# Weight pieces gated by landings, two-tile MLP groups, loads spread over a round and split transposes in a fused attention and MLP kernel

## The chip, the cores and the metric

The kernel runs on one core of one Trainium2 chip. The metric is the device time of one execution in microseconds (us), measured outside the profiler. Ratios below are the mean time of one kernel's fast runs over that of the other kernel's fast runs of the same rounds on the same chip, so they are not quite the ratio of the medians that I quote. A run counts as slow when it lies more than 1.5% above the fastest run of its kernel on that chip; slow runs are in the medians but not in the ratios. A point below is one per cent of before's time. Profiles are single executions; their span (253.97 us before) is some 1.7 us shorter than the device time of the same execution (255.67 us). So the profiled execution of before lay 1.7 us above the median of its runs.

In the lines of profiles PE is TensorE's matmuls, PEld its weight loads, DVE VectorE, ACT ScalarE, POOL GpSimd; SPq and ACTq are SyncE and ScalarE issuing transfers, and L92 is line 92 of that kernel. A bracket gives the idle time before an instruction and what ended it. A transfer lands when the engines that wait for it may go on. The granted clock is the share of TensorE's full clock in the profile's records, which begin 19.3 us into the span before; where there is no record it is printed as full.

## The reference, cut to what matters

A decaying linear attention over 4 batches, 8 heads, 768 positions and head size 64 (float32), and then, on its output x of 3,072 rows by 512, a normalization and a two-layer MLP with a residual:

```python
# attention, per block of 64 positions, state carried from block to block
intra = einsum('bhic,bhjc->bhij', qb, kb) * Dmask          # decayed causal mask
out   = einsum('bhij,bhjd->bhid', intra, vb) + einsum('bhid,bhde->bhie', qb * lam_pow, kv_state)
kv_state = lam_block * kv_state + einsum('bhsd,bhse->bhde', kb * rev_pow, vb)
...
# MLP on x = out, laid out as (batch, position, head*dim)
xn = (x - mean) / sqrt(var + 1e-6) * g_ln
y  = x + maximum(xn @ w_ch1, 0) @ w_ch2                    # 512 -> 2048 -> 512
```

## The kernel before

The work is cut into 12 *windows* of 256 rows (two tiles of 128), with the four batches in turn. For each window SyncE loads k, q and v (512 KB each), mostly GpSimd turns k, q and v into bf16 (q and v scaled), k and q are transposed (`kqT`; by TensorE in the first three windows, by a transposing DMA afterwards), TensorE makes the state products (`pk`), the scores (`sc`) and the attention output (`po`), VectorE and ScalarE normalize it (`x`, `xc`), `xc` is transposed (`xT`), and the MLP runs on *groups* of tiles. The weights come as eight pieces, four of each layer, through GpSimd's queue, which turns float32 into bf16 on the way (before's page: 4.19 MB moved by that queue, for 8.39 MB of float32 weights).

```python
def load_window(u, after_pool=False, parts=1):      # all three loads of a window at once, on SyncE
    ...
def load_w1(c): nc.gpsimd.dma_start(w1[c], ...)     # one piece of the first layer's weights
def load_w2(c): nc.gpsimd.dma_start(w2[c], ...)
...
sizes = [2, 2, 2, 2, 2, 2, 4, 4, 4]                 # tiles of each MLP group
...
# the front: order in which weights and windows are asked for
load_w1(0); load_window(1, after_pool=True); ...
load_w1(1); load_w1(2); ... in_q(1, nc.gpsimd); in_v(1, nc.gpsimd)
load_w1(3); load_window(2, after_pool=True); load_w2(0)
...
load_w2(1); load_w2(2); load_w2(3)                  # issued a few us later, long before window 2 is needed
...
# the plan: a list of MLP steps (first layer: 8 or 4 matmuls, second layer: 4), with attention put in between
def s1_s3(u):                                       # one round: state products and scores of u, output of u-1
    kv(u); scores(u, 0); av(u - 1, range(NP)); inter(u - 1, 0, fence=False)
    new_state(u, 0, nc.gpsimd); mask(u, 0); reader(u - 1); new_state(u, 1, nc.gpsimd)
def ahead_of(u):
    for f, w in ((transpose_dma, u + 1), (load_window, u + 3), (p0, u + 2)): ...   # p0: GpSimd's preparation
for at, j, rest in ((40, 5, 4), (56, 6, 4), (65, 7, 4), (73, 8, 4), ...):
    after[at] = [(s1_s3, j)]
    after[at + rest] = [(s2_s4, j), (p4, j - 1)]    # p4: the x transposes of window j-1
    after[at - 1] = [(ahead_of, j)]
```

## Time and profile before

| | before |
|---|---|
| device time, median of 3 | 253.99 us (253.97 to 254.61) |
| TensorE busy / idle until its last matmul | 212.4 us / 36 us |
| TensorE takes up q of window 2 | 48.47 us |
| round 6 starts | 117.24 us |
| last matmul ends | 248.3 us |
| mean granted clock of TensorE | 0.941 |

The row "takes up q" is the start of the run of seven transposes after the wait for window 2's q:

```profile
48.47 0.93 PE L183 MATMUL tp<-ident,kq 128*128 128x128 bf16 x7 [0.71 <-POOL kq L169]
```

A round is the attention work put in between the MLP steps for one window; round 6 is that of window 6. From the place above on, the order of the MLP steps is the same in both kernels up to round 6. The other lines stand in the prediction.

### The profile page before, as it was taken

Reading aid. Unit: us, or ns where it says so; the run is one execution under the profiler, and the core shown is the slowest. Engines: PE = TensorE matmul, PEld = TensorE weight load, DVE = VectorE, ACT = ScalarE, POOL = GpSimd, SP = SyncE. Lnnn points to the kernel's source line nnn. Section 1 sums busy time; section 2 is a strip of 40 time slices with the busy share of each in tenths; the row PEclk is TensorE's granted clock in tenths of the full one; section 3 lists DMA queues with packets and bytes.
Section 4 is the critical chain, followed back from the end, with each engine's and each line's share of the span. In section 5 each row is a group of like instructions: output and inputs, shape, how many; then the busy total and the mean of one; then the engine's idle time right before and its main releaser. Section 6 shows DMA issues by size and latency. Waiting matters only on the chain.

```text
span 254.0 us, 6453 instructions
## 1 busy us (share of the span) xinstructions
PE 212.4 (84%) x2829; PEld 123.9 (49%) x2848; DVE 101.7 (40%) x216; ACT 85.0 (33%) x154; POOL 74.2 (29%) x92
## 2 busy tenths in 40 slices
PE   1664892499999949699978996989999899999991
PEld 0454681364476437448546742545445444444440
DVE  2762431037535712354558271261562605300121
ACT  5446174131035003313504511462115632067000
POOL 5705600538608456461073725000000000000000
PEclk9999799579999967799999997999999999999998
DMA  5997799579799989986999999326043110430042
GB/s 155 239 259 138 118 207 218 124 197 290 127 270 245 264 150 317 229 119 103 211 193 235 243 265 151 61 43 85 18 108 85 24 23 9 116 83 3 0 108 57
DMA packets 75276, 37.38 MB, mean 147 GB/s; under 512 B 30960, under 2 KB 72176, under 8 KB 75248
## 3 DMA queue, kind: packets, MB, share of 16 engines
q1 hardware_dynamic: 70880, 32.78, 61.6%
q0 software_dynamic: 4224, 4.19, 10.1%
q8 instruction: 22, 0.36, 0.6%
q14 instruction: 6, 0.05, 0.1%
q10 hardware_dynamic: 144, 0.00, 0.0%
HBM read 27.53 MB, written 6.29 MB: 133 GB/s over the span
## 4 chain that ended last, share of the span: by engine, by line
PE 54%; DMA 24%; POOL 8%; DVE 5%; SPq 4%; issue 2%; ACT 1%; DVEq 0%; ACTq 0%; POOLq 0%
PE pm L383 26%; PE pm L357 22%; DMA qin<-in_q_dram 10%; DMA vin<-in_v_dram 10%; POOL vb L174 3%; DMA kin<-in_k_dram 3%; POOL kq L169 2%; DMA xT<-xc 2%; SPq L189 2%; SPq L75 2%; PE po L270 2%; DVE stats L307 2%; PE sc L205 2%; POOL Sn L235 1%; DVE xc L309 1%
## 5 line engine op out<-in xcount | busy, mean ns | idle before, releaser
L357 PE MATMUL pm<-xT,w 128*128 128x256 bf16 (+1 forms) x539 | 93.6, 332 | 9.4 <-DMA xT<-xc 5.5
L383 PE MATMUL pm<-w,hT 128*128 128x512 bf16 x370 | 85.3, 380 | 1.1 <-issue 0.5
L360 ACT ACTIVATE hT<-pm 128x512 bf16<-128x512 f32 x92 | 53.6, 597 | 82.0 <-PE pm L357 81.9
L357 PEld LDWEIGHTS <-w 128*128 128x128 bf16 x544 | 55.0, 105 | 42.1 <-DMA xT<-xc 6.4
L383 PEld LDWEIGHTS <-hT 128*128 128x128 bf16 x384 | 36.7, 98 | 42.8 <-issue 0.6
L404 DVE SCALAR_TENSOR_TENSOR o<-pm,rstd,x 128x512 f32<-128x512 f32 (+1 forms) x25 | 18.0, 725 | 48.0 <-PE pm L383 31.2
L215 DVE TENSOR_TENSOR mA<-sc,keep 128x512 bf16<-128x512 f32 x44 | 28.2, 682 | 22.5 <-PE sc L205 22.4
L169 POOL TENSOR_TENSOR kq<-qin,lam_q 128x512 bf16<-128x512 f32 (+1 forms) x24 | 24.0, 1019 | 27.2 <-DMA qin<-in_q_dram 27.1
L235 POOL TENSOR_TENSOR Sn<-Stmp,lam_s 128x256 bf16<-128x256 f32 x16 | 9.8, 612 | 60.0 <-DVE Stmp L239 51.3
L174 POOL TENSOR_TENSOR vb<-vin,lam_v 128x1024 bf16<-128x1024 f32 (+1 forms) x13 | 23.1, 1782 | 7.2 <-DMA vin<-in_v_dram 7.2
L307 DVE BATCH_NORM_STATS2 stats<-x 128x6 f32<-128x512 f32 x20 | 13.8, 691 | 21.3 <-ACT x L305 21.2
L183 PE MATMUL tp<-ident,kq 128*128 128x128 bf16 x48 | 6.4, 279 | 16.9 <-POOL kq L169 8.3
L305 ACT COPY x<-po 128x512 f32<-128x512 f32 x20 | 10.9, 590 | 28.3 <-PE po L283 23.7
L309 DVE SCALAR_TENSOR_TENSOR xc<-po,mv,g_row 128x512 bf16<-128x512 f32 x24 | 18.0, 750 | 2.0
L239 DVE TENSOR_TENSOR Stmp<-pk,Sn 128x256 f32<-128x256 f32 x16 | 6.7, 418 | 27.6 <-PE pk L229 20.8
L161 POOL CAST kq<-kin 128x512 bf16<-128x512 f32 x16 | 9.3, 611 | 22.4 <-DMA kin<-in_k_dram 22.4
L183 PEld LDWEIGHTS <-kq 128*128 128x128 bf16 x48 | 4.0, 122 | 18.8 <-DVE kq L161 9.4
L270 PE MATMUL po<-vb,mA 64*64 64x64 bf16 x768 | 10.3, 199 | 1.9 <-issue 1.3
L205 PE MATMUL sc<-kqT 64*64 64x128 bf16 x352 | 10.0, 227 | 1.5 <-ACT kqT L184 0.9
L270 PEld LDWEIGHTS <-mA 64*64 64x64 bf16 x768 | 9.0, 110 | 3.5 <-issue 2.6
L184 ACT COPY kqT<-tp 128x1024 bf16<-128x1024 bf16 (+1 forms) x7 | 5.7, 830 | 13.7 <-PE tp L183 13.7
L334 ACT ACTIVATE std<-mv,eps_t 128x2 f32<-128x2 f32 x12 | 3.6, 298 | 19.7 <-DVE mv L308 19.7
(54 smaller groups left out, 90.3 us busy)
## 6 DMA issues: line engine op xcount, KB each, us to landing
kin<-in_k_dram SPq DMA_DIRECT2D x11, 512.0 KB, 5.4
qin<-in_q_dram SPq DMA_DIRECT2D x11, 512.0 KB, 6.2
vin<-in_v_dram SPq DMA_DIRECT2D x11, 512.0 KB, 8.0
out_dram<-o SPq DMA_DIRECT2D x22, 256.0 KB, 3.5
w<-in_moe_w_ch_dram POOLq DMA_DIRECT2D x8, 512.0 KB, 11.3
kin<-in_k_dram SPq DMA_DIRECT2D x2, 256.0 KB, 4.7
qin<-in_q_dram SPq DMA_DIRECT2D x2, 256.0 KB, 5.1
vin<-in_v_dram SPq DMA_DIRECT2D x2, 256.0 KB, 5.4
```

What stands on the lines that cost most here:

```text
L169: eng.tensor_tensor(dst[:, :, :, j], src[:, :, :, j], lq[:, :, :, j:j + 1].to_broadcast([128, n, 2, D]), op=ALU.mult)
L174: eng.tensor_tensor(st[u]["vb"][:, hs], qkv_in[u]["v"][:, hs], lam_v[:, hs, :, None].to_broadcast([128, n, 2, D]), op=ALU.mult)
L205: nc.tensor.matmul(sc[e][half[ab], i, jk, :], lhsT=kT[half[e], 2 * hf + i, jk, half[ab]], rhs=qT[half[e], 2 * hf + i, :, half[ab]], start= ...
L215: nc.vector.tensor_tensor(s[f"mA{hf}"][:, e], s[f"sc{hf}"][e], kp[:, None, :, :].to_broadcast([128, 2, 2, 128]), op=ALU.mult)
L235: eng.tensor_tensor(dst, src, lam_s[:, :, None].to_broadcast([128, NP, D]), op=ALU.mult)
L270: nc.tensor.matmul(s["po"][ab][half[jq], 2 * p + e, :], lhsT=s[f"mA{p // 2}"][half[ab], e, p % 2, j, half[jq]], rhs=s["vb"][half[ab], 2 * ...
L307: nc.vector.bn_stats(stats, po if early else x)
L309: nc.vector.scalar_tensor_tensor(xc, in0=po, scalar=mv[:, 0:1], in1=g_row, op0=ALU.subtract, op1=ALU.mult)
L357: nc.tensor.matmul(pm[:, b, :], lhsT=w1[n // W2K][:, kk, (n % W2K) * 128:(n % W2K + 1) * 128], rhs=xT_of[g][:, kk, 0:N], start=(b == 0 and ...
L360: nc.scalar.activation(hT[:, u * NB:(u + 1) * NB, 0:N], pm, ACT.Relu)
L383: nc.tensor.matmul(acc[i], lhsT=hT[:, kk, i * 128:(i + 1) * 128], rhs=w2[kk // W2K][:, kk % W2K, :], start=(kk == 0), stop=(kk == KB - 1))
L404: nc.vector.scalar_tensor_tensor(o[:, ab, sl], in0=a[:, sl], scalar=rstd[:, ab:ab + 1], in1=x[:, ab, sl], op0=ALU.mult, op1=ALU.add)
```

## The change

Its intent is to have neither weights nor inputs wait for the other in the first 50 us, and to have nothing wait in the rounds. Cut to its core:

```diff
-    sizes = [2, 2, 2, 2, 2, 2, 4, 4, 4]
+    sizes = [2] * NU                                  # and GT = 2
@@ the front
+    def behind(tile_ap):                              # GpSimd reads one column of a tile: it waits for its landing
+        seen_p = wk.tile([128, 1], F32, tag="seen_p", name="seen_p")
+        nc.gpsimd.tensor_copy(seen_p, tile_ap)
     open_window(0)
-    load_w1(0)
-    load_window(1, after_pool=True)
+    load_window(1)
...
+    behind(w1[0][:, 0, 0:1])
     load_w1(1)
+    in_q(1, nc.gpsimd)
     load_w1(2)
+    load_w1(3)
     in_v(1, nc.gpsimd)
+    load_w2(0)
+    behind(w1[2][:, 0, 0:1])
     load_window(2, after_pool=True)
...
-    load_w2(1)
-    load_w2(2)
-    load_w2(3)
+    behind(w2[0][:, 0, 0:1])
+    load_w2(1)
+    in_q(2, nc.gpsimd)
+    load_w2(2)
+    in_v(2, nc.gpsimd)
+    load_w2(3)
@@ k and q transposed by two DMAs
-        nc.sync.dma_start_transpose(s["kqT"]..., s["kq"]...)
+        for a in range(2):
+            nc.sync.dma_start_transpose(s["kqT"][:, a]..., s["kq"][:, a]...)
@@ the rounds
+    for j in range(6, NU):
+        at = 56 + 16 * (j - 6)
+        add(at - 1, (transpose_dma, j + 1))
+        add(at, (s1_s3, j))
+        add(at + 2, (p0, j + 2))                      # behind the state sums of round j, no longer in front
+        add(at + 4, (s2_s4, j), (p4, j - 1))
+        for n, name in zip((3, 7, 10), "kqv"):
+            add(at + n, (load_one, j + 3, name))      # one load at a time
@@ the tail: the last tile's second layer in two halves of columns, each stored on its own,
@@ the stores from SyncE and ScalarE
```

(Cut: rounds 2 to 5, which are spread in the same way by hand; the first window's order; in the rounds, the second state sum ahead of the second half of the mask.)

More of the change, by code (lines that the diff above doesn't have):

```diff
@@ L39 @@
     KB = DF // 128
-    GT = 4
+    GT = 2
     NWC = 4
@@ L64, in source, with load_one @@
         return src[b, hs, cc * W:(cc + 1) * W, :].rearrange("h (p j) d -> p h (j d)", j=2)
+    def load_one(u, name):
+        got = inp.tile([128, H, 2 * D], F32, tag=name + "in", name=name + "in")
+        nc.sync.dma_start(got, source(dict(k=k, q=q, v=v)[name], u, slice(0, H)))
+        qkv_in.setdefault(u, {})[name] = got.rearrange("p h (j d) -> p h j d", j=2)
     def load_window(u, after_pool=False, parts=1):
@@ L128 @@
     lam_v = const.tile([128, H, 2], F32)
-    for j in range(2):
-        nc.scalar.activation(lam_v[:, :, j], lnlam, ACT.Exp, scale=e_v[:, j:j + 1])
     lam_c = const.tile([128, H], F32)
-    nc.scalar.activation(lam_c, lnlam, ACT.Exp, scale=float(C))
     lam_s = const.tile([128, NP], F32)
@@ L188, in transpose_dma @@
         s["kqT"] = wk.tile([128, 2, NP, 2, 128], BF16, tag="kqT", bufs=3, name="kqT")
-        nc.sync.dma_start_transpose(s["kqT"].rearrange("p a b j t -> p (a b j) t"),
-                                    s["kq"].rearrange("p a b j e d -> p (a b j e d)"))
+        for a in range(2):
+            nc.sync.dma_start_transpose(s["kqT"][:, a].rearrange("p b j t -> p (b j) t"),
+                                        s["kq"][:, a].rearrange("p b j e d -> p (b j e d)"))
     def scores(u, hf, early=False):
@@ L209, in scores, with mask @@
         s[f"sc{hf}"] = sc
-    def mask(u, hf):
+    def mask(u, hf, heads=(0, 1)):
         s = st[u]
         kp = keep.rearrange("p a b t -> p a (b t)")
-        for e in range(2):
+        for e in heads:
             nc.vector.tensor_tensor(s[f"mA{hf}"][:, e], s[f"sc{hf}"][e],
@@ L345, in mlp @@
         N = n_t * 128
-        NB = max(1, GT // n_t)
+        NB = 4 // n_t
         def m1(u):
@@ L379, in m2 @@
             t = groups[g][i]
+            if t == 2 * NU - 1:
+                w = DM // 2
+                if part % 2 == 0:
+                    acc[i] = mm_tile([128, w], F32, "pm2h")
+                z = part // 2
+                for kk in range(part % 2 * 8, part % 2 * 8 + 8):
+                    nc.tensor.matmul(acc[i], lhsT=hT[:, kk, i * 128:(i + 1) * 128],
+                                     rhs=w2[kk // W2K][:, kk % W2K, z * w:(z + 1) * w],
+                                     start=(kk == 0), stop=(kk == KB - 1))
+                if part % 2 == 1:
+                    finish_half(t, acc.pop(i), z, w)
+                return
             if part == 0:
@@ L398, in finish, with finish_half @@
         rows = out[b, cc * W:(cc + 1) * W, :].rearrange("(c p j) d -> j p c d", c=2, j=2)
-        last = u == NU - 1
-        n_p = 2 if last and ab == 1 else 1
-        w = DM // n_p
-        for z in range(n_p):
-            sl = slice(z * w, (z + 1) * w)
-            nc.vector.scalar_tensor_tensor(o[:, ab, sl], in0=a[:, sl], scalar=rstd[:, ab:ab + 1], in1=x[:, ab, sl],
-                                           op0=ALU.mult, op1=ALU.add)
-            if last:
-                for j in range(2):
-                    nc.sync.dma_start(rows[j][:, ab, sl], o[half[j], ab, sl])
-        if ab == 1 and not last:
+        nc.vector.scalar_tensor_tensor(o[:, ab], in0=a, scalar=rstd[:, ab:ab + 1], in1=x[:, ab],
+                                       op0=ALU.mult, op1=ALU.add)
+        if u == NU - 1:
+            for j in range(2):
+                nc.sync.dma_start(rows[j][:, ab], o[half[j], ab])
+        elif ab == 1:
             for j in range(2):
                 nc.sync.dma_start(rows[j], o[half[j]])
-    sizes = [2, 2, 2, 2, 2, 2, 4, 4, 4]
+    def finish_half(t, a, z, w):
+        u, ab = divmod(t, 2)
+        x, rstd = x_keep[u]
+        cc, b = divmod(u, B)
+        o = o_of[u]
+        sl = slice(z * w, (z + 1) * w)
+        rows = out[b, cc * W:(cc + 1) * W, :].rearrange("(c p j) d -> j p c d", c=2, j=2)
+        nc.vector.scalar_tensor_tensor(o[:, ab, sl], in0=a, scalar=rstd[:, ab:ab + 1], in1=x[:, ab, sl],
+                                       op0=ALU.mult, op1=ALU.add)
+        for j, eng in enumerate((nc.sync, nc.scalar)):
+            eng.dma_start(rows[j][:, ab, sl], o[half[j], ab, sl])
+    sizes = [2] * NU
     groups = [list(range(sum(sizes[:i]), sum(sizes[:i + 1]))) for i in range(len(sizes))]
@@ L423 @@
     HA, HB = slice(0, 4), slice(4, 8)
+    def behind(tile_ap):
+        seen_p = wk.tile([128, 1], F32, tag="seen_p", name="seen_p")
+        nc.gpsimd.tensor_copy(seen_p, tile_ap)
     open_window(0)
-    seen_k = const.tile([128, 1], F32)
-    nc.gpsimd.tensor_copy(seen_k, qkv_in[0]["k"][:, 0, 0, 0:1])
-    load_w1(0)
-    load_window(1, after_pool=True)
-    in_k(0, nc.vector, HA)
-    transpose_pe(0, 0, (0, 1), nc.vector)
-    nc.vector.tensor_tensor(lam_q[:, :, 1], lam_q[:, :, 0], lam_b, op=ALU.mult)
-    in_q(0, nc.gpsimd, HA)
-    in_k(0, nc.vector, HB)
+    load_window(1)
+    in_k(0, nc.vector, HA)
+    transpose_pe(0, 0, (0, 1))
+    for j in range(2):
+        nc.scalar.activation(lam_v[:, :, j], lnlam, ACT.Exp, scale=e_v[:, j:j + 1])
+    nc.scalar.activation(lam_c, lnlam, ACT.Exp, scale=float(C))
+    nc.vector.tensor_tensor(lam_q[:, :, 1], lam_q[:, :, 0], lam_b, op=ALU.mult)
+    in_q(0, nc.vector, HA)
+    in_k(0, nc.gpsimd, HB)
+    load_w1(0)
     in_q(0, nc.vector, HB)
+    transpose_pe(0, 0, (2, 3), nc.vector)
     lam_cp = lam_c.rearrange("p (a two) -> p a two", two=2)
@@ L438 @@
         nc.vector.tensor_copy(lam_s[half[e]], lam_cp[half[e], :, e])
+    transpose_pe(0, 1, (0, 1))
+    transpose_pe(0, 1, (2, 3))
+    sqrt_first = const.tile([128, 1], F32)
+    nc.scalar.activation(sqrt_first, eps_t, ACT.Sqrt)
     in_v(0, nc.gpsimd, HA)
     in_v(0, nc.gpsimd, HB)
-    transpose_pe(0, 0, (2, 3))
-    transpose_pe(0, 1, (0, 1))
     scores(0, 0)
     mask(0, 0)
-    transpose_pe(0, 1, (2, 3))
+    scores(0, 1, early=True)
+    mask(0, 1)
     kv(0)
-    scores(0, 1, early=True)
     new_state(0, 0, nc.gpsimd)
-    mask(0, 1)
-    sqrt_first = const.tile([128, 1], F32)
-    nc.scalar.activation(sqrt_first, eps_t, ACT.Sqrt)
     av(0, (0, 1, 2))
@@ L455 @@
     av(0, (3,), (0,))
+    open_window(1)
+    norm(0, 0, early=True)
+    behind(w1[0][:, 0, 0:1])
     load_w1(1)
+    in_q(1, nc.gpsimd)
     load_w1(2)
-    open_window(1)
-    in_k(1, nc.scalar)
-    norm(0, 0, early=True)
-    in_q(1, nc.gpsimd)
+    load_w1(3)
     in_v(1, nc.gpsimd)
-    load_w1(3)
+    load_w2(0)
+    behind(w1[2][:, 0, 0:1])
     load_window(2, after_pool=True)
-    load_w2(0)
     m1a, m2a = mlp(0)
@@ L475 @@
     to_xT(0, 0)
+    in_k(1, nc.scalar)
     inter(0, 1)
     norm(0, 1, early=True)
-    transpose_pe(1, 0, (0, 1, 2, 3))
-    keep_x(0, (0,))
     m1a.tile(0, 0)
     to_xT(0, 1)
+    transpose_pe(1, 0, (0, 1, 2, 3))
     transpose_pe(1, 1, (0, 1, 2, 3))
+    m1a.tile(0, 1)
+    keep_x(0, (0,))
     keep_x(0, (1,))
-    m1a.tile(0, 1)
     scores(1, 0)
@@ L488 @@
     mask(1, 1)
-    load_w2(1)
-    load_w2(2)
-    load_w2(3)
+    rstd_of(0)
+    m1s(m1a, 1)
     kv(1, "po")
@@ L494 @@
     st[1]["tmp"] = state_sum(1, 1)
-    rstd_of(0)
-    m1s(m1a, 1)
     av(1, (0, 1, 2, 3))
@@ L502 @@
     norm(1, 1, early=True)
-    open_window(2)
-    in_k(2, nc.vector)
-    in_q(2, nc.gpsimd)
-    in_v(2, nc.gpsimd)
-    load_window(3, after_pool=True)
-    load_window(4)
     m1s(m1a, 2, 1, 2)
@@ L513 @@
     m1s(m1a, 3, 1, 2)
+    open_window(2)
+    in_k(2, nc.vector)
     m1b.tile(0, 0)
@@ L517 @@
     rstd_of(1)
+    behind(w2[0][:, 0, 0:1])
[4 more added lines that the diff above has]
+    load_w2(3)
+    load_window(3, after_pool=True)
+    load_window(4)
     def p0(u, k_eng=None):
@@ L537, in s1 @@
         new_state(u, 0, nc.gpsimd)
-        mask(u, 0)
+        mask(u, 0, (0,))
         new_state(u, 1, nc.gpsimd)
+        mask(u, 0, (1,))
     def s2(u):
@@ L568, in s1_s3 @@
         new_state(u, 0, nc.gpsimd)
-        mask(u, 0)
+        mask(u, 0, (0,))
+        new_state(u, 1, nc.gpsimd)
+        mask(u, 0, (1,))
         reader(u - 1)
-        new_state(u, 1, nc.gpsimd)
     def s2_s4(u):
@@ L588 @@
         plan += [(m2, i, part) for i in range(len(groups[g])) for part in range(KB // 4)]
-    def ahead_of(u):
-        for f, w in ((transpose_dma, u + 1), (load_window, u + 3), (p0, u + 2)):
-            if w < NU:
-                f(w)
-    after = {0: [(transpose_pe, 2, 0, (0, 1, 2, 3))], 1: [(transpose_pe, 2, 1, (0, 1, 2, 3))],
-             2: [(new_state, 0, 1, nc.gpsimd), (new_state, 1, 1, nc.gpsimd)],
-             4: [(s1b, 2)], 5: [(s0, 2)], 6: [(s2, 2)], 7: [(p0, 3, nc.vector)], 9: [(s3, 2)], 11: [(s4, 2), (p4, 2), (transpose_dma, 3), (load_window, 5)],
-             17: [(p0, 4)], 24: [(s1, 3)], 26: [(transpose_dma, 4), (load_window, 6), (s2, 3)],
-             28: [(s3, 3), (p0, 5)], 30: [(s4, 3), (p4, 3)], 33: [(s1, 4)], 35: [(transpose_dma, 5), (load_window, 7)], 36: [(s2, 4)],
-             37: [(p0, 6)]}
@@ L602, with add @@
-    for at, j, rest in ((40, 5, 4), (56, 6, 4), (65, 7, 4), (73, 8, 4), (89, 9, 4), (105, 10, 4), (121, 11, 4)):
-        after[at] = [(s1_s3, j)]
-        after[at + rest] = [(s2_s4, j), (p4, j - 1)]
-        after[at - 1] = [(ahead_of, j)]
-    after[135] = [(s3, 11)]
-    after[139] = [(s4, 11), (p4, 11)]
+    after = {}
+    def add(at, *steps):
+        after.setdefault(at, []).extend(steps)
+    add(0, (transpose_pe, 2, 0, (0, 1, 2, 3)))
+    add(1, (transpose_pe, 2, 1, (0, 1, 2, 3)))
+    add(2, (new_state, 0, 1, nc.gpsimd), (new_state, 1, 1, nc.gpsimd))
@@ new lines @@
+    add(4, (s1b, 2))
+    add(5, (s0, 2))
+    add(6, (s2, 2))
+    add(7, (p0, 3, nc.vector))
+    add(9, (s3, 2))
+    add(11, (s4, 2), (p4, 2), (transpose_dma, 3))
+    for n, name in zip((12, 14, 16), "kqv"):
+        add(n, (load_one, 5, name))
+    add(17, (p0, 4))
+    add(24, (s1, 3))
+    add(26, (s2, 3))
+    add(26, (load_one, 6, "k"))
+    add(28, (s3, 3), (p0, 5))
+    add(29, (s4, 3), (p4, 3), (transpose_dma, 4))
+    add(31, (load_one, 6, "q"))
+    add(32, (load_one, 6, "v"))
+    add(37, (transpose_dma, 5))
@@ new lines @@
+    add(38, (load_one, 7, "k"))
+    add(41, (s1, 4))
+    add(42, (p0, 6))
+    add(43, (s2, 4), (load_one, 7, "q"))
+    add(45, (s3, 4), (load_one, 7, "v"))
+    add(46, (s4, 4), (p4, 4))
+    add(46, (transpose_dma, 6))
+    add(50, (s1, 5))
+    add(51, (p0, 7))
+    add(52, (s2, 5))
+    for n, name in zip((48, 50, 52), "kqv"):
+        add(n, (load_one, 8, name))
+    for j in range(6, NU):
+        at = 56 + 16 * (j - 6)
+        if j + 1 < NU:
+            add(at - 1, (transpose_dma, j + 1))
+        add(at, (s1_s3, j))
+        if j + 2 < NU:
+            add(at + 2, (p0, j + 2))
+        add(at + 4, (s2_s4, j), (p4, j - 1))
+        if j + 3 < NU:
+            for n, name in zip((3, 7, 10), "kqv"):
+                add(at + n, (load_one, j + 3, name))
@@ L608 @@
+    add(150, (s3, NU - 1))
+    add(154, (s4, NU - 1), (p4, NU - 1))
     for i, (f, *a) in enumerate(plan):
```

## The prediction

Marked cuts below are clauses that gave rules of the hardware without a trace that shows them; what was measured beside them stays. The sum: 254.0 - 12.8 - 6.8 + 1.2 - 1.9 = 233.7. Two terms in it are my estimates, and before's trace has for them: 1.6 us from the end of the last packet (252.3) to the end of the span for the "some 1.5" of a landing, and 2.75 us from the end of the last issue (251.2) for the "about 2.5" of the tail. The 2,048 bytes read per weight packet are the float32 weights, 8.39 MB of the 27.53 MB on the page's HBM line, over 4,096 packets.

> **What bounds the kernel now.** I read the page's busy line, its table of 40 slices, then the chain of waits in order of time, the waits of TensorE, the issue queue of SyncE, and last the windows.
>
> ```profile
> PE 212.4 (84%) x2829; PEld 123.9 (49%) x2848; DVE 101.7 (40%) x216; ACT 85.0 (33%) x154; POOL 74.2 (29%) x92
> PE   1664892499999949699978996989999899999991
> PEclk9999799579999967799999997999999999999998
> DMA  5997799579799989986999999326043110430042
> ...
> q1 hardware_dynamic: 70880, 32.78, 61.6%
> q0 software_dynamic: 4224, 4.19, 10.1%
> ```
>
> One slice is 6.35 us. Counted from 0, TensorE is full in most slices but not in the first eight and not in 14, 16 and 24. The DMA row is well filled from the start to slice 24 and loose afterwards: up to about 159 us two resources share the bound, from then on TensorE alone has it. The chain of waits names the two long front waits, window 1's v and window 2's q:
>
> ```profile
> 7.86 16.21 DMA vin<-in_v_dram
> ...
> 27.33 18.96 DMA qin<-in_q_dram
> 46.29 0.07 issue
> 46.37 2.06 POOL kq L169 x2
> ...
> 117.31 0.44 PE pk L229 x32
> ```
>
> An undisturbed q load takes 6.2 us from issue to landing (median of the page); this one took 19. All five remaining weight pieces had been issued with it, four of them just behind:
>
> ```profile
> 26.77 0.12 POOL L70 MEMSET kin<- 128x1 f32 x1
> 26.81 2.97 POOL L87 DMA_DIRECT2D w<-in_moe_w_ch_dram  x4
> 46.37 2.05 POOL L169 TENSOR_TENSOR kq<-qin,lam_q 128x512 bf16<-128x512 f32 x2 [16.58 <-DMA qin<-in_q_dram]
> ```
>
> TensorE waits 6.1 us for that q (until 47.47). The windows, by stretch, give the rest (columns: stretch, length, busy of PE, PEld, DVE, ACT, POOL with counts, granted clock, DMA share, GB/s):
>
> ```profile
> 85.00:93.00 8.00, 4.72 (x36) 2.17 (x36) 3.78 (x7) 0.00 (x0) 6.21 (x7) 0.88 1.36 217
> 93.00:104.00 11.00, 8.93 (x176) 6.81 (x175) 2.19 (x6) 3.58 (x6) 5.91 (x7) 0.78 1.09 238
> 121.00:137.00 16.00, 14.22 (x265) 8.91 (x265) 9.71 (x21) 4.12 (x9) 6.30 (x7) 1.00 1.27 200
> 137.00:155.00 18.00, 14.40 (x220) 9.06 (x219) 10.20 (x22) 6.00 (x12) 9.67 (x11) 1.00 1.16 242
> 172.00:220.00 48.00, 46.98 (x574) 22.79 (x579) 20.81 (x44) 14.34 (x28) 1.22 (x2) 1.00 0.26 57
> ```
>
> Length minus PE busy is TensorE's idle time: 3.28, 2.07, 1.78, 3.60, 1.02 us here, 0.22 in 104 to 121 and 0.71 in 155 to 172. Sum after 85 us: 12.7. A DMA share above 1 stands beside all four large gaps, and 0.26 beside the small one, so those look like waits for traffic or for what is queued behind it.
>
> [...] q of window 2, on SyncE's queue, took 18.96 us beside GpSimd's weights. [...] A weight packet here carries 1,024 written bytes (2,048 read), an input packet 512; [...] in the packet records a quarter-megabyte of input took about 3.6 us while weights ran, 0.9 us alone. [...] 24 matmuls of 256 columns took 5.30 us after the wait at 92 us, 2.62 us warm at 71 us. [...] 226 ns for 512 columns, 109 to 116 for 256.
>
> **The change part by part.**
>
> 1. *Front.* Before, GpSimd issues w1's pieces 1 and 2 at 10.8 us, beside window 1, and five pieces around window 2. Now window 1 is issued at once, w1(1) only after w1(0) has landed, w1(2), w1(3), w2(0) among q and v of window 1; window 2 follows the landing of w1(2); w2(1) follows the landing of w2(0), w2(2) the q and w2(3) the v of window 2. Eight weight pieces take 10.1% of 254 = 25.7 us of all engines, 3.2 us each; input packets 73.0 us by the packet records, 6.1 per window. Estimate: w1(0) lands at about 16, w1(1) 22, w1(2) 27.5. So window 2 is issued near 28, hardly earlier than the 26.9 of before, but beside two pieces (7 us) rather than five (16). Its q then lands near 39.5; GpSimd takes 2.05 us. TensorE resumes at about 41.5 instead of 48.5: **-7.0 us at that place**.
>
> 2. *Is that gain kept?* This is the step in which I chose. From there to round 6 (its state products run at 117.3 us in the chain) the DMA engines carry nearly as much as TensorE. Their work ahead of round 6: eight windows 48.7, g_row 1.0, weights 25.7, four k/q transposes at 3.74 = 15.0 and six x transposes at 0.94 = 5.6 (28,672 packets hold 52.4 us), six outputs at 0.98 = 5.9 (23.4 us over 24): 101.9, from about 2.5 us on, plus some 1.5 for the last landing: 106. TensorE alone, from 41.5: before it needed 117.3 - 48.5 = 68.8, of which 0.8 + 0.3 + 3.3 + 2.1 + 0.2 = 6.7 idle and about 3.5 at half clock: 58.6, so round 6 at about 100. The truth lies between, since not all of that traffic has to be in front and the transposes' average includes congestion: I take 104.5. **-12.8 us** in all up to there, the 7.0 included.
>
> 3. *Rounds 6 to 11.* Before: 1.78 + 3.60 + 0.71 + 1.02 = 7.1 us idle, and 1.7 at half clock (16 matmuls in 5.30 us at 154.8 instead of 3.61). The groups of four needed two windows' xT at once; groups of two need one and come ten steps of 0.9 us after its transposes. Loads are issued one at a time; the GpSimd work of window j+2 stands behind the state sums of round j rather than in front, where it held the sum for a late v (1.90 us at 131.50, with 0.58 behind it). By step 2's terms a window needs 6.1 + 3.7 + 1.9 + 2.0 = 13.7 us of DMA against some 16.4 of TensorE (7.4 + 6.9 for the group, 2.1 attention), so DMA no longer limits. Recovered 8.8 less 2.0 that I leave for waits on xT (half the slack of nine us is the normalization on VectorE and ScalarE): **-6.8**.
>
> 4. *Costs of two-tile groups.* 192 matmuls of 512 columns become 384 of 256: 192 x (2 x 116 - 226) = **+1.2**. Weight loads (98 ns) stay beside matmuls of 109 or more. The relu has as many instructions as before, 0.6 us per 0.9 of TensorE.
>
> 5. *Tail.* TensorE ends at 248.3, the program at 254.0: two VectorE halves, four issues one after another on SyncE (2.38), landing. Now half the last tile leaves before the last sixteen matmuls, and the last two issues are on two queues: 0.48 + 0.55 + about 2.5 rather than 5.7. Less 0.25 for halving the last matmuls: **-1.9**. Splitting the k and q transposes adds nine issues on SyncE, which isn't the bound: 0.
>
> Sum: 254.0 - 12.8 - 6.8 + 1.2 - 1.9 = 233.7; I say **233.5**.
>
> **The rivals.** (a) DMA stays the bound to round 6. For it: share 0.9 to 1.36 there, and the 101.9 us of traffic, of which the change removes nothing. Then round 6 starts at 106 to 108 and the time is 236 to 238. (b) DMA hides entirely and TensorE is fed from 41.5: 229. (c) A new wait takes the old one's place: GpSimd, in program order, now stops for landed weights in front of in_q, in_v and the states; a late v of window 2 would hold back w2(3) and window 3 after it, and the second layer waits on weights. Against it: w2(3) would land near 53, and the first product that needs it comes near 57. It would give back 4 to 8 us: 238 to 242. (d) Rounds of 16 short steps are too tight for xT, 1 to 2 us of wait in each of six rounds: 236 to 242. Before, from the end of the state products at 181.8 to the landed xT was 7 us, under the nine now given, which speaks against it.
>
> **Range and chances.** (b) with a good tail gives 227, (a) and part of (d) 241: range **227 to 241**. To miss 2% (248.9) both the front and the gaps must fail, against a visible 18.96 us wait and 12.7 us of idle TensorE. Faster **0.94**, same **0.05**, slower **0.01**.
>
> **What would show it.** Step 1: the wait for window 2's q under 13 us, TensorE back at 41 to 42. Step 2: round 6's state products near 104; at 100 the DMA was no bound, at 108 it was the only one. Step 3: under 3 us of TensorE idle from there to its last matmul, clock 1.00 throughout. Step 4: TensorE's 256-column matmuls 110 to 116 ns apart, warm. Step 5: under 4 us from the last matmul to the end. I am wrong if GpSimd shows long waits for w, if second-layer matmuls wait for a weight piece, or if xT waits appear in every round.

## The result, and the profile after

The changed kernel takes 230.3 us (median of 4, 229.45 to 231.11) against 253.98 (median of 4, 252.61 to 254.61). The ratio of the fast runs is 0.907, 95% interval 0.902 to 0.913. I had said 233.5, range 227 to 241.

The page of the changed kernel, the same rows that the prediction shows of before:

```profile
PE 204.7 (89%) x3056; PEld 139.4 (61%) x3056; DVE 101.4 (44%) x216; ACT 84.9 (37%) x154; POOL 73.4 (32%) x93
PE   0647697989999999698999999999999999999992
PEclk9999999999999999999999999999999999999999
DMA  5996999999999999999999699695193212311303
```

Counted from 0, TensorE is full from slice 9 on but for slices 16 and 18 and the last. It does the same arithmetic in 7.7 us less busy time, mainly because the clock row has no dip any more (mean 1.00 instead of 0.941). That holds from the first clock record on: before it, 16 matmuls of 128 columns at 18.15 us take 1.89 us, against 1.06 at 21.63. The DMA row has lost its dips too: it is full from slice 4 to 21, then loose.

The chain of waits, columns start, length, what (the first two against 27.33 to 46.37 of before, the last against 117.31):

```profile
27.69 9.36 DMA qin<-in_q_dram
...
37.12 2.05 POOL kq L171 x2
...
100.30 0.38 PE pk L232 x32
```

Window 2's q was issued no earlier than before (27.69 against 27.33 us), but was there after 9.4 us rather than 19. What GpSimd does in between, from its timeline, shows why; the weight pieces w2(1) to w2(3) are the lines of L92:

```profile
33.51 0.74 POOL L92 DMA_DIRECT2D w<-in_moe_w_ch_dram  x1 [0.27 <-issue]
37.12 2.05 POOL L171 TENSOR_TENSOR kq<-qin,lam_q 128x512 bf16<-128x512 f32 x2 [2.87 <-DMA qin<-in_q_dram]
39.12 0.80 POOL L92 DMA_DIRECT2D w<-in_moe_w_ch_dram  x1
39.95 1.91 POOL L176 TENSOR_TENSOR vb<-vin,lam_v 128x1024 bf16<-128x1024 f32 x1
41.80 0.80 POOL L92 DMA_DIRECT2D w<-in_moe_w_ch_dram  x1
```

One piece goes out after w2(0) has landed, one after q, one after v. In the packet records w2(1) moves its first packet at 36.3 us, when q is practically in (its last packets start at 35.0). TensorE takes up q here:

```profile
39.23 0.56 PE L185 MATMUL tp<-ident,kq 128*128 128x128 bf16 x7 [0.78 <-POOL kq L171]
```

The stretches of TensorE (stretch, length, busy of PE, PEld, DVE, ACT, POOL with counts, granted clock, DMA share, GB/s). First of the kernel before, from q of window 2 on:

```profile
48.50:59.00 10.50, 10.45 (x116) 6.79 (x118) 4.01 (x8) 3.40 (x5) 5.20 (x7) 0.76 0.66 172
71.20:97.40 26.20, 22.86 (x331) 14.85 (x335) 12.04 (x23) 7.44 (x13) 12.16 (x14) 0.88 1.10 243
97.40:117.30 19.90, 17.61 (x264) 11.76 (x267) 8.12 (x17) 5.93 (x11) 11.02 (x12) 0.90 0.93 183
117.30:248.40 131.10, 123.78 (x1532) 64.36 (x1544) 52.08 (x111) 44.61 (x83) 20.09 (x23) 0.99 0.55 105
```

and of the changed kernel:

```profile
49.40:60.80 11.40, 10.31 (x55) 4.53 (x52) 6.23 (x13) 0.89 (x3) 7.86 (x8) 1.00 1.17 254
80.70:100.30 19.60, 17.42 (x321) 10.88 (x324) 11.35 (x23) 5.55 (x10) 12.42 (x14) 1.00 1.22 221
117.30:149.90 32.60, 32.20 (x501) 21.76 (x502) 15.61 (x33) 11.85 (x22) 11.81 (x13) 1.00 0.96 178
149.90:182.20 32.30, 32.08 (x482) 21.52 (x484) 15.19 (x32) 11.85 (x22) 6.21 (x7) 1.00 0.64 90
182.20:224.90 42.70, 42.53 (x521) 29.54 (x520) 13.87 (x30) 15.21 (x28) 0.61 (x1) 1.00 0.23 55
```

From 117 us on TensorE idles 0.40 + 0.22 + 0.17 us in 108 us. What idle time is left lies in front: 15.1 us in the first 39.3, 1.1 and 2.2 us in the first two stretches above, and 1.0 us at 106.3.

The account by milestones. Each interval is taken between the same two places of the program:

| interval | before | after | change |
|---|---|---|---|
| start to q of window 2 taken up | 48.5 | 39.2 | -9.2 |
| from there to the start of round 6 | 68.8 | 61.0 | -7.8 |
| round 6 to the last matmul's end | 131.1 | 124.6 | -6.5 |
| last matmul's end to the end of the span | 5.6 | 4.1 | -1.6 |
| span | 254.0 | 228.9 | -25.1 |

(The medians differ by 23.7 us only, since the profiled execution of before was slower than its median.)

The tail, from the timelines; before:

```profile
248.33 0.88 DVE L404 SCALAR_TENSOR_TENSOR o<-pm,rstd,x 128x256 f32<-128x256 f32 x2 [2.70 <-PE pm L383]
248.84 2.38 SPq L408 DMA_DIRECT2D out_dram<-o  x4
```

after:

```profile
223.65 2.25 ACTq L433 DMA_DIRECT2D out_dram<-o  x2
224.88 0.48 DVE L430 SCALAR_TENSOR_TENSOR o<-pm2h,rstd,x 128x256 f32<-128x256 f32 x1 [1.26 <-PE pm2h L389]
```

One half of the last tile is added and stored while the other is still being multiplied, so one VectorE step and half of the stores follow the last matmul instead of two and all. No run undoes the tail alone; its share is read from these profiles.

### The profile page after: what moved, and what is told of

It reads as the page before. It is cut to its first block, busy times and chain, and to the rows that moved or that the text cites. A ratio compares the mean times of both kernels' runs of the same rounds, so it can differ in the third digit from the quotient of the medians.

```text
span 228.9 us, 6911 instructions
## 1 busy us (share of the span) xinstructions
PE 204.7 (89%) x3056; PEld 139.4 (61%) x3056; DVE 101.4 (44%) x216; ACT 84.9 (37%) x154; POOL 73.4 (32%) x93
## 3 DMA queue, kind: packets, MB, share of 16 engines
HBM read 27.53 MB, written 6.29 MB: 148 GB/s over the span
## 4 chain that ended last, share of the span: by engine, by line
PE 52%; DMA 24%; POOL 8%; issue 6%; DVE 5%; ACT 2%; SPq 1%; DVEq 0%; POOLq 0%
PE pm L360 24%; PE pm L398 22%; DMA w<-in_moe_w_ch_dram 7%; DMA qin<-in_q_dram 6%; DMA kin<-in_k_dram 6%; POOL kq L171 3%; DMA xT<-xc 2%; DMA kqT<-kq 2%; DVE stats L310 2%; POOL kq L163 2%; POOL vb L176 2%; PE po L273 2%; PE pm2h L389 2%; DVE xc L312 1%; PE pk L232 1%
## 5 line engine op out<-in xcount | busy, mean ns | idle before, releaser
L360 PE MATMUL pm<-xT,w 128*128 128x256 bf16 x736 | 87.3, 273 | 3.4 <-DMA xT<-xc 1.3
L363 ACT ACTIVATE hT<-pm 128x512 bf16<-128x512 f32 x92 | 54.6, 596 | 91.7 <-PE pm L360 91.6
L398 PE MATMUL pm<-w,hT 128*128 128x512 bf16 x368 | 83.0, 379 | 0.4
L360 PEld LDWEIGHTS <-w 128*128 128x128 bf16 x736 | 69.8, 98 | 15.7 <-issue 3.0
L398 PEld LDWEIGHTS <-hT 128*128 128x128 bf16 x368 | 34.9, 98 | 41.6 <-ACT hT L363 2.6
L414 DVE SCALAR_TENSOR_TENSOR o<-pm,rstd,x 128x512 f32<-128x512 f32 x23 | 17.1, 745 | 35.4 <-PE pm L398 35.2
L171 POOL TENSOR_TENSOR kq<-qin,lam_q 128x512 bf16<-128x512 f32 x22 | 22.6, 1048 | 10.4 <-DMA qin<-in_q_dram 10.2
L185 PE MATMUL tp<-ident,kq 128*128 128x128 bf16 x48 | 5.3, 261 | 8.1 <-DVE kq L163 5.5
L163 POOL CAST kq<-kin 128x512 bf16<-128x512 f32 (+1 forms) x18 | 10.1, 588 | 4.4 <-DMA kin<-in_k_dram 4.4
L208 PEld LDWEIGHTS <-kqT 64*64 64x64 bf16 x384 | 7.3, 111 | 3.6 <-issue 3.3
```

Source lines behind the costliest of these rows:

```text
L163: (eng.copy if eng is nc.scalar else eng.tensor_copy)(dst[:, :, :, j], src[:, :, :, j])
L171: eng.tensor_tensor(dst[:, :, :, j], src[:, :, :, j], lq[:, :, :, j:j + 1].to_broadcast([128, n, 2, D]), op=ALU.mult)
L208: nc.tensor.matmul(sc[e][half[ab], i, jk, :], lhsT=kT[half[e], 2 * hf + i, jk, half[ab]], rhs=qT[half[e], 2 * hf + i, :, half[ab]], start= ...
L360: nc.tensor.matmul(pm[:, b, :], lhsT=w1[n // W2K][:, kk, (n % W2K) * 128:(n % W2K + 1) * 128], rhs=xT_of[g][:, kk, 0:N], start=(b == 0 and ...
L363: nc.scalar.activation(hT[:, u * NB:(u + 1) * NB, 0:N], pm, ACT.Relu)
L398: nc.tensor.matmul(acc[i], lhsT=hT[:, kk, i * 128:(i + 1) * 128], rhs=w2[kk // W2K][:, kk % W2K, :], start=(kk == 0), stop=(kk == KB - 1))
```

## The experiments

Twelve kernels ran. In this section "the changed kernel" has the ratio 0.907 (interval 0.902 to 0.913), measured with its own rounds on its own chip; the experiments ran on others, where before took 255.3 to 255.5 us in the median. So I compare ratios to before, and differences under half a per cent between runs of different chips are not taken for real.

| run | median us | ratio to before, 95% interval |
|---|---|---|
| front only | 246.92 | 0.957 (0.948 to 0.967) |
| rounds only | 240.40 | 0.942 (0.935 to 0.949) |
| last three weight pieces at once | 240.12 | 0.940 (0.933 to 0.947) |
| no outputs of windows 0 to 2 | 228.81 | 0.895 (0.889 to 0.900) |
| groups of four at the end | 237.00 | 0.929 (0.923 to 0.934) |
| loads of a window together | 240.67 | 0.940 (0.932 to 0.948) |
| preparation ahead of the state sums | 237.63 | 0.929 (0.922 to 0.936) |
| one transpose for k and q | 230.85 | 0.903 (0.897 to 0.909) |
| first weight piece earlier | 229.23 | 0.897 (0.891 to 0.902) |
| k of window 3 prepared later | 230.63 | 0.905 (0.899 to 0.910) |
| first outputs deferred | 231.23 | 0.905 (0.900 to 0.910) |
| the last three together | 229.70 | 0.899 (0.895 to 0.903) |

All gave the right result but the fourth, which is wrong on purpose. Slow were two of the four runs of front only, one of four with the loads together, and one of six with the first piece earlier.

**Are the two halves of the change independent?** Theory: the gain at the front moves everything behind it. Rival: it is lost in the old rounds' waits for the DMA, and the halves need each other. Two kernels, each with one half:

```diff
@@ front only: the kernel before, with
-    (its code from the first window to the start of the plan)
+    (the changed kernel's code for the same part)
@@ rounds only: the changed kernel, with
-    (its code from the first window to the start of the plan)
+    (the code of before for the same part)
```

> The kernel before with only the prefix of the changed one (landing waits, order of weight pieces and of windows 1 and 2); rounds, groups and tail as before. Theory 'front moves everything behind it': TensorE resumes at window 2's transposes at 39 to 41 us and the whole gain of 9 us is kept: about 245 us. Theory 'two halves need each other' (the early start is eaten by the gaps of the old rounds, which wait for the DMA anyway): 249 to 254 us, the wait on xT near 90 us grows from 3 us to 6 or more.

> The changed kernel with the prefix of before: rounds, spread loads, groups of two, split transposes and tail are new, the front is old. TensorE resumes at 48.5 us as before. Theory 'additive': it gives 25 less 9 = 15 to 16 us, about 238 to 239 us. Theory 'two halves need each other': the DMA, less loaded with TensorE late, lets the new rounds start as early as they can, and the late front costs under 6 us: 231 to 236 us; or the new rounds gain little: over 243.

Front only: the q transposes at 39.0 us, round 6 at 106.4 instead of 117.2, 4.3% saved. The rival's sign did appear; from the waits of TensorE (us in total, times, longest), where before has 5.5, 2, 3.2:

```profile
PE pm L354 <- DMA xT<-xc: 7.6, 3, 4.1
```

But it is 2 us more of waiting, not the whole gain. Rounds only: q taken up at 48.4, round 6 at 109.6, 5.8% saved. The product of the two ratios is 0.901, and the whole change has 0.907, which is within the two intervals: the halves add up as far as these runs can tell, and the rival falls.

**What in the front does it?** Theory: fewer weight pieces on the engines beside window 2. Rival: window 1's earlier start and the order of the pieces.

```diff
     behind(w1[2][:, 0, 0:1])
     load_window(2, after_pool=True)
+    load_w2(1)
+    load_w2(2)
+    load_w2(3)
...
-    behind(w2[0][:, 0, 0:1])
-    load_w2(1)
     in_q(2, nc.gpsimd)
-    load_w2(2)
     in_v(2, nc.gpsimd)
-    load_w2(3)
```

> The changed kernel with the last three weight pieces issued in one go right behind the issue of window 2, as in before, rather than one each behind the landing of w2(0), of q and of v. Theory 'fewer weight pieces beside window 2 are the front gain': window 2's q lands at 45 to 47 us instead of 37, the time is 236 to 239. Theory 'the gain comes from the start of window 1 and the order of the pieces': q lands under 40 us, time under 233.

GpSimd's timeline of this run:

```profile
27.25 2.22 POOL L92 DMA_DIRECT2D w<-in_moe_w_ch_dram  x3
45.09 2.05 POOL L171 TENSOR_TENSOR kq<-qin,lam_q 128x512 bf16<-128x512 f32 x2 [15.62 <-DMA qin<-in_q_dram]
```

With nothing moved but three issues (and one landing wait gone with them), q is there at 45.1 instead of 37.1 us, TensorE takes it up at 47.2 instead of 39.2, round 6 starts 8.0 us later and the span is 7.6 us longer. So 8.0 of the front's 9.2 us are those three pieces, and nearly all of it reaches the end. The times on this chip say the same: with the three pieces put back the kernel is as slow (0.940) as with the whole front of before (rounds only, 0.942), so the rival is worth nothing that shows. The packet records of before show what weights do to an input. With weights running (32.9 to 43.8 us), 512 input packets of 512 bytes took 3.60 to 3.69 us three times over, and 503 to 505 weight packets moved in each of these stretches; with none running (53.9 to 62.8 us) 512 input packets took 0.75 to 0.93. At 2,048 bytes read for a weight packet, four fifths of the bytes read in the first stretches were weights, which nobody needed yet.

**Is the DMA the bound up to round 6?** This was my rival (a), and (b) its opposite.

```diff
-        elif ab == 1:
+        elif ab == 1 and u > 2:                 # outputs of windows 0 to 2 are never stored
```

> The changed kernel without the twelve output transfers of the first three windows (wrong result on purpose: those rows are never written). It takes 5.8 us of packet time off the DMA engines between 66 and 108 us. Theory 'DMA-bound up to round 6' (rival a): round 6 starts 3 to 5 us earlier, the time is 225 to 227. Theory 'TensorE is fed, the DMA only just keeps up': round 6 moves by less than 1.5 us, and only the 1.3 us wait on xT near 97 us goes: 228.5 to 230.3.

Round 6 starts at 97.9 instead of 100.2, of which 0.5 is there already at q of window 2, before any output. So 5.8 us of packet time less moves round 6 by some 1.8 us: neither the 3 to 5 of a bound nor the under 1.5 of a free DMA. Most of the DMA's time there is hidden, not all of it. The ratio is 1.2 points better than the changed kernel's (which ran on another chip); 0.5 us of it, as said, has another cause.

**Which part of the rounds?** Four kernels, each with one part undone.

```diff
@@ groups of four at the end, with before's places for rounds 6 to 11
-    sizes = [2] * NU
+    sizes = [2, 2, 2, 2, 2, 2, 4, 4, 4]
@@ loads of a window together (the same for windows 5 to 8)
-            for n, name in zip((3, 7, 10), "kqv"):
-                add(at + n, (load_one, j + 3, name))
+            add(at + 3, (load_window, j + 3))
@@ preparation ahead of the state sums
-            add(at + 2, (p0, j + 2))            # behind (s1_s3, j)
+            add(at - 1, (p0, j + 2))            # in front of it
@@ one transpose for k and q
-        for a in range(2):
-            nc.sync.dma_start_transpose(s["kqT"][:, a]..., s["kq"][:, a]...)
+        nc.sync.dma_start_transpose(s["kqT"]..., s["kq"]...)
```

> The changed kernel with three groups of four tiles at the end (as in before, with the places of before in the plan for rounds 6 to 11), all else as changed: spread loads, order on GpSimd, split transposes, front, tail. Theory 'groups of two remove the wait for two windows' xT': gaps of 1 to 4 us come back at the starts of the four-tile groups, the time is 233 to 237 us. Rival 'the loads and the order on GpSimd did it': within 1 us of the changed kernel, 229.5 to 231.5, or even 1 us less through the longer matmuls.

It costs 2.1 points, within what the theory gave, but only partly by its cause. TensorE's timeline:

```profile
114.30 0.22 PE L273 MATMUL po<-vb,mA 64*64 64x64 bf16 x4 [2.81 <-issue]
114.65 5.19 PE L398 MATMUL pm<-w,hT 128*128 128x512 bf16 x16
138.65 3.61 PE L360 MATMUL pm<-xT,w 128*128 128x512 bf16 x16 [1.03 <-DMA xT<-xc]
```

The wait on the second window's xT is there, at 138.65, with 1.0 us; ScalarE's relu holds TensorE twice for 0.6 each. The largest piece is a gap of 2.81 us inside a run of output products, for which the profile names no releaser, and the slower matmuls after it (5.19 us for 16 that take 3.6 otherwise). More on this gap at the end. The edit also brings back before's distances between rounds, and the loads move with them. That groups of two with their places are better than groups of four with before's is shown; that it is mainly the wait for two windows is not.

> The changed kernel with the three loads of a window issued together, at the place where k's is now, ahead of the x transposes on SyncE's queue. Theory 'spreading keeps transposes from queueing behind 6 us of loads': xT lands 3 to 4 us later in each round, which uses up the slack of nine steps, waits on xT of 1 to 2 us in several rounds, 233 to 238 us. Rival 'the DMA has slack after round 6': under 1 us, at most 231.

It costs 3.3 points, the largest of the four. Its profile is slow, so I read from it the kind of the wait and not the size:

```profile
PE pm L360 <- DMA xT<-xc: 9.1, 3, 4.6
```

In the changed kernel the same line is 1.3 us, once. On SyncE's queue of this run k, q and v of window 9 are issued at 112.5 to 115.6 us and the x transposes of window 5 at 115.75 behind them, though VectorE had their input ready at 113.2; in the changed kernel the transposes follow k alone at 108.7, and q and v come after them. The rival, that the DMA has slack after round 6, falls: there is slack in amount (a share of 0.64 from 149.9 to 182.2 us in the changed kernel), but on the queue these transposes were issued only when the three loads had been.

> The changed kernel with GpSimd's preparation of window j+2 in front of the state sums of round j in rounds 6 to 9, as in before. Theory 'order on GpSimd': a late load holds up the sum and with it the inter-chunk products; 2 to 4 us in these rounds, 232 to 234.5. Rival 'the loads come early enough now': under 1 us; the preparation then costs the sum only the rest of its own 5 us, hidden by the state sum's slack.

It costs 2.2 points, more than I had expected. The waits are not spread over the rounds; it is nearly one wait, in round 6. GpSimd's and TensorE's timelines:

```profile
107.65 1.90 POOL L176 TENSOR_TENSOR vb<-vin,lam_v 128x1024 bf16<-128x1024 f32 x1 [1.03 <-DMA vin<-in_v_dram]
109.51 0.61 POOL L238 TENSOR_TENSOR Sn<-Stmp,lam_s 128x256 bf16<-128x256 f32 x1
```

```profile
110.64 1.89 PE L360 MATMUL pm<-xT,w 128*128 128x256 bf16 x8 [6.27 <-DVE Stmp L242]
```

GpSimd waits for window 8's k, q and v in turn before it makes the state that round 6 asked for at 101 us; the second state sum on VectorE waits for that state, and TensorE for the accumulator which the sum reads. After 6.27 us of this it is slower (8 matmuls of 256 columns in 1.89 us rather than 1.04). The rival, that loads come early enough now, falls.

> The changed kernel with one transposing DMA for k and q of a window as in before. My prediction gave the split 0. Theory 'no effect': within 0.7 us. Rival: k's half can start before q is prepared, and the transpose of round 3, 4 or 5 is on the path, so one transfer costs 1 to 3 us.

The ratio is 0.903, against 0.907 for the changed kernel: no effect that these runs could show, as predicted. The split transposes land sooner each (median 4.9 us from issue instead of 5.9), but the second of a pair is issued behind the first, whose issue takes 1.9 us (median).

**Is there something better than both?** Four kernels aim at the waits which the changed kernel still has.

```diff
@@ first weight piece earlier
-    in_k(0, nc.gpsimd, HB)
+    behind(qkv_in[0]["k"][:, 0, 0, 0:1])
     load_w1(0)
+    in_k(0, nc.gpsimd, HB)
@@ k of window 3 prepared later: at 7 only q and v; k on VectorE at 11, behind (s4, 2)
@@ first outputs deferred: stores of windows 0 to 2 at 118, 134, 148 of the plan, six buffers o,
@@ and v of window 7 loaded behind the x transposes of window 4
```

> A try to go beyond the changed kernel: the first weight piece is issued behind the landing of k's first half rather than after GpSimd has prepared k's second half, some 2 us earlier. TensorE waits 2.0 us for that piece at 18 us now. Theory 'front still moves everything': the wait goes, the later pieces and window 2 come 1 to 2 us earlier, 228 to 229.5 us beside 230.3. Rival 'round 6 is DMA-paced': the front is earlier but round 6 stays at 100, 230 to 231.

> The changed kernel with VectorE's preparation of k of window 3 placed behind the normalization of window 2. In the changed kernel it stands in front, waits 4.2 us for k's landing, and TensorE then waits 1.1 us for VectorE's reader behind it. Theory: that 1.1 us goes and stays gone, 229 to 229.5 us; rival: taken back by the DMA before round 6, 230 to 230.5.

> The changed kernel with the outputs of windows 0 to 2 kept on chip and issued in rounds 9 to 11, where the DMA share is 0.2 to 0.6, and v of window 7 issued behind the x transposes of window 4. Without these outputs round 6 came 2.3 us earlier and the span was 1.4 us shorter (another chip). Theory: that is kept while the result stays right, 228.5 to 229.3 us, no wait on xT at 97 us. Rival: the late outputs lengthen xT in rounds 9 to 11, 230 to 231.

> All three together. If they add up, 226 to 227.5 us; if the DMA before round 6 takes back the first two, as with defer_outs alone, 228.5 to 229.5.

None is clear of the noise. The earlier piece has the best ratio, 0.897, and its interval (to 0.902) just touches that of the changed kernel, but the two did not run on one chip and its profile was slow; I do not claim it. The deferred stores, which I expected to keep most of what the run without them had won, keep nothing that shows (0.905): round 6 comes at 98.9, 1.3 us earlier, and a wait of 1.2 us on xT before round 7 takes nearly all of it back. The later k is the most instructive. The changed kernel waits here for VectorE, and this one should not; TensorE's timelines, changed kernel first:

```profile
51.82 0.31 PE L286 MATMUL po<-Sn,kqT 64*64 64x64 bf16 x8 [1.09 <-DVE seen L297]
```

```profile
60.68 2.78 PE L360 MATMUL pm<-xT,w 128*128 128x256 bf16 x24 [1.25 <-DMA xT<-xc]
```

The 1.09 us wait is gone, and 1.25 us have come up nine us later, before group 2, which then starts at 60.68 instead of 60.83: the x transposes of window 2 are issued at 54.28 us, behind six loads of windows 3 and 4 that take SyncE from 42.46 to 54.2. With all three together round 6 comes at 96.6 us, 3.6 earlier, and a wait of 1.64 us on xT before round 7 (there is none in the changed kernel) takes half of it back. So in these profiles most of a microsecond won in front of round 7 was paid again in a wait on xT. I take from it that a further gain has to take traffic out of the first 100 us or change its order, not start TensorE earlier; no run shows that.

## Why the prediction was right

*Step 1, the front: -7.0 predicted, -9.2 measured.* The mechanism was the predicted one: window 2 issued at 27.3, "hardly earlier than the 26.9 of before", and beside fewer pieces; the run with three pieces put back shows 8.0 us for it. The term that was mis-sized was q's landing: I put it near 39.5, and it came at 37.1. I had counted two pieces, 7 us, beside window 2. In the packet records w1(3) was already moving at 26.1 us, w2(0) was through at 32.4, and the first input packet moved at 31.3: only the last 60 or so weight packets went beside it, and k and q then had the engines to themselves until 35.0. The first weight piece was two us later than I had it (18.1 instead of 16); TensorE waited 2.0 us for it, but window 2's issue came as estimated.

*Step 2, is it kept: round 6 predicted at 104.5, measured at 100.2.* This is the step in which I chose, and I chose too high. I had 100 from TensorE alone and 106 from the DMA. The second bound was wrong in kind. I had summed the times of packets (101.9 us) as if the engines took them one after another. They overlap: the share is 1.22 in the stretch before round 6, and the packets that start in the first 100.3 us of the changed kernel take 105.8 us by the records. The shares of 1.09 to 1.36 stood in the prediction's own fence. The run without early outputs says how much of a bound the DMA is: 1.8 us of 5.8.

On the TensorE side the term at half clock was too small. I had put it at 3.5 us from q of window 2 to round 6. Busy time in that interval is 68.8 - 5.9 = 62.9 us before and 61.0 - 3.3 = 57.7 after, for the same products: 5.2 us. Only 2.6 us of idle time was removed, so the clock made up two thirds of this interval's gain. Not all of the 5.2 comes from waits inside the interval: the clock record of before has half clock from 43.2 to 53.5 us, so some 2.5 of it (an estimate, half of the 5.0 us from 48.5 to 53.5) is still the price of the wait for q. After the 3.23 us wait inside it, 24 matmuls took 2.51 us longer than the next 24:

```profile
92.12 5.30 PE L357 MATMUL pm<-xT,w 128*128 128x256 bf16 x24 [3.23 <-DMA xT<-xc]
98.85 2.79 PE L357 MATMUL pm<-xT,w 128*128 128x256 bf16 x24
```

Two readings in the prediction's sum were loose: of its 6.7 us of idle time 0.8 lies in front of the interval, which starts at 48.5, and it set 5.30 us of the timeline against 2.62 of the chain, where the timeline has 2.78.

*Step 3, the rounds: -6.8 and +1.2 of step 4, so -5.6; measured -6.5.* TensorE's idle time from round 6 to its last matmul went from 7.3 us to 1.8 (1.0 before 108 us, 0.8 after 117), under the 3 us that I had named as the test, and its clock was 1.00. That the loads, the order on GpSimd and the size of the groups each matter is shown by the three runs, 3.3, 2.2 and 2.1 points. Those add up to more than the rounds' whole gain of 5.8%; each of them alone is enough to make TensorE wait, and the matmuls after a wait were slower (8 in 1.89 us rather than 1.04 after the 6.27 us). What was wrong in the reasoning is the sentence "so DMA no longer limits": in amount, yes; but three loads in a row ahead of a transpose on the same queue cost more than any other part (3.3 points).

*Step 4, the two-tile groups: +1.2 predicted; some 0.4 by an estimate from the traces.* 64 matmuls of 256 columns take 6.99 us in the chain, 109 each; in before the best long run of 512 columns is 29 in 6.26, 216 each, which is 2 less than two of the small ones. 192 times 2 ns are 0.4 us. No run isolates it. I had compared a slower run of small ones (116) with a middling run of large ones.

*Step 5, the tail: -1.9 predicted, -1.6 measured.* From the last matmul's end it is 4.1 us instead of 5.6; from the end of the last issue it took 3.0 us (225.9 to 228.9), not my 2.5. The split of the transposes: 0 predicted, none shown.

*Rivals.* (a) and (b) both hold in part, as said. (c) did not come, though one sign that I had named for it did: GpSimd stands 14.8 us in waits for landed weights (longest 7.2), but no second-layer matmul waits for a piece. (d) did not come: there is one wait on xT, 1.3 us, before round 6, and none later.

*Luck.* The mechanism was right, but steps 1 to 4 all gave too little. In spans I was 4.8 us off (233.7 against 228.9); between the medians it is 3.2, because the 254.0 from which I started was a profile 1.7 us slower than before's median.

## What to carry to other kernels

When two kinds of load share the DMA engines and one is needed later, don't issue it early because its queue is free: here 512 input packets took 0.9 us alone and 3.6 with weights running, and three weight pieces issued with window 2 put its q off from 37.1 to 45.1 us. Let a cheap read of a landed tile hold the issue back. When TensorE waits, count the slower matmuls after it too: here the 24 and 16 matmuls behind waits of 3.23 and 2.25 us took 2.5 and 1.7 us longer, and in one run 8 matmuls behind several short waits took 1.89 us rather than 1.05 (the last section has the numbers). And in a steady round look at what stands in front of each transpose in its queue before adding up bytes (three loads there cost 3.3 points), and do not take a sum of packet times for a lower bound (packets with 105.8 us of it started in the first 100.3 us).

## What else the traces show

- The clock after waits. In before's clock record the granted clock is 0.50 in five stretches between the first record (19.3 us) and the last matmul, 27.3 us in all, and 1.00 elsewhere. The wait of TensorE in front of each: 2.22 us from 23.86 (0.50 from 26.15, for 3.41 us), 6.08 from 41.38 (from 43.22, 10.24), 3.23 from 88.89 (from 91.01, 6.83), 2.07 from 101.64 (from 104.66, 3.41) and 2.25 from 152.57 (from 155.86, 3.41). Waits of 1.46 us from 38.15 and 1.25 from 128.99 had no such stretch behind them. The changed kernel has none after its first record (21.0 us); its longest wait there is 1.30 us, from 96.21. Short waits differ: behind 0.78, 0.53 and 0.34 us between 24.3 and 27.6 us with all three together, 8 matmuls of 256 columns took 1.89 us at 28.80 and 1.05 at 30.98; behind the same three in the changed kernel they took 1.05 at 28.84. Behind 0.78 and 1.66 us with one transpose for k and q, 24 such matmuls took 4.17 us at 97.87; behind 0.78 and 1.45 in the run with groups of four, 2.79 at 97.04. How much idle time it takes is not shown by these. Executions of one kernel differ in their mean clock (0.993 and 1.00 among the four with one transpose).
- Packet times overlap: the sum of the packets' times in a stretch, as a share of 16 engines, was up to 1.36 (85 to 93 us in before), and I mis-sized a bound by it.
- Shares of two queues: in before from 32.9 to 43.8 us, weight packets (2,048 bytes read, 1,024 written) and input packets (512 bytes) moved in nearly equal number, 503 to 505 against 512 in each 3.6 us, so weights had some four times the bytes read.
- Two gaps of TensorE have no releaser: 2.81 us from 111.49 in the run with groups of four, 1.00 us from 106.33 in the changed kernel. In the changed kernel a packet of 16,384 bytes of the instruction queue starts 1.5 us before the gap (at 104.81, lasting 1.20). Most of the 24 such packets of that run are followed by no gap, and no run varied this, so it is a coincidence in time and not a shown cause.
